# GpSimd's drain moved into the experts' arms, small arms' splits all on VectorE, two weight loads moved behind the first tail's gathers

## The chip, the cores and the metric

The kernel runs on one core of a Trainium2 chip. Its engines are TensorE (PE in the profile, with its weight loads as PEld), VectorE (DVE), ScalarE (ACT), GpSimd (POOL) and SyncE (SP, which only issues DMAs here). Each engine works through its own list of instructions in order and waits for the others by semaphores. The metric is the device time of one execution in microseconds (us); lower is better.

## The reference

Attention over 8 batches and 8 heads (512 local and 32 global positions, a window of 32 on either side) gives 4352 token rows of 512 numbers. A mixture of eight experts then works on them:

```
do_compute = x @ w_skip > 0
xc = x[do_compute];  logits = xc @ w_gate;  e_idx = argmax(logits)
gate_w = softmax(logits)[e_idx]
for e in range(8):
    h = maximum(xc[e_idx == e] @ w1[e], 0)          # 512 -> 1024
    y[e_idx == e] = gate_w * (h @ w2[e])            # 1024 -> 512
out = x.copy();  out[do_compute] = xc + y
```

With the inputs drawn, 1980 tokens are computed, and the experts 0 to 7 get 395, 171, 153, 289, 173, 371, 253 and 175 of them.

## The kernel before, in words

**Attention and routing** take the first 230 us or so. Each token's row is written to `out`, and per expert a list of row numbers and gates is written to a table in DRAM (`lst`).

**An expert** takes its tokens in groups of 128 rows. A gather (line 128) is one indirect DMA on GpSimd's queue that fetches 128 rows of 2 KB from `out`; `gather(...)` issues two of them. TensorE turns the rows (`turn_x`, line 221), and multiplies them with w1 (`first` at line 881 for 256 tokens, `first_small` at line 903 for up to 192) into three PSUM banks used in turn, ScalarE and VectorE turning each result into a high and a low part of `hc` (lines 887, 888, 908, 910). Then TensorE multiplies with w2 (`second`, line 920, 24 matmuls for each 128 tokens; `second_small`, line 931). VectorE weighs the result by the gate and adds the row (`weigh`, line 1000), and GpSimd scatters it back to `out` (`scatter`, line 993).

**The weights** come in float32. Each expert's 4 MB are loaded in eight pieces of 512 KB (lines 176 and 179) into a ring of six `raw` tiles. `split` makes a high part on ScalarE (line 192) and a low part by a subtraction (line 195) on VectorE or, for one piece of each small arm, on GpSimd. `roll(e)` splits one piece and issues the next load (`fetch`). Six rolls stand in an expert's first stage (behind its hidden blocks f = 0, 1, 2, 4, 5, 6), two in its second. SyncE does not wait for these places: it issues the loads in order, each as soon as its tile is free.

**The arms.** Each expert from 1 on has two branches. `few` (at most 192 tokens: experts 1, 2, 4 and 7 here) and `wide` (3, 5 and 6; 3 and 5 have over 256 tokens and also run `tail`). Every engine takes the branch by itself, from a count that it has loaded. Where GpSimd skips an arm, it raises the semaphores that the arm's DMAs would have raised (INC_SWDGE_SEM in the profile). Both arms start with `begin` (line 1207): VectorE weighs the last expert's remaining group into the single tile `ylast`, and GpSimd gathers the next expert's rows into the tile which that group has just left. These rows are turned by `turn_next` between the first and the second stage. A wide arm also gathers its own second list into `xgs[2]` for `tail`. Behind the arms come a scatter of `ylast`, `join` and `weigh` for the second group, a scatter of `yo`, the drain of GpSimd (line 1249), and the second stage of the first 128 tokens.

Expert 0 (lines 1139 to 1197) has its own course: the first stage, `second` twice, with the hooks `rest` (line 1029: gathers of its own third group and of expert 1's rows, and up to four weight loads from GpSimd's queue) and `flags` (line 1155: turns the third group, its "first tail"), then its arms.

The order of each engine's instructions is written out by hand (`manual_schedule`), so that each list stands as the code reads.

Of the kernel before, what the change touches and what calls it, by code (L numbers as in the profile page):

```python
# [45 lines left out]
def kernel(  # L46
# [12 lines left out]
    nc = tc.nc  # L59
# [6 lines left out]
    def ps_s(name):  # L66
        return ps.tile([P, 512], F32, tag="s", name=name, bufs=3)
# [4 lines left out]
    def ps_v(name):  # L72
        return ps.tile([P, 512], F32, tag="v", name=name, bufs=2)
# [16 lines left out]
    six = const.tile([P, E, 2, NSUB], U32, name="six")  # L90
# [9 lines left out]
    xs = []  # L100

    def apart(ins, group, *groups):
        i = getattr(ins, "ins", ins)
        for g in groups:
            tc.declare_no_dep(i, group=g, reason="rows are distinct")
        tc.add_to_no_dep_group(group, i)
# [19 lines left out]
    def gather(xg, gidx, nrow=NT):  # L126
        for t in range(NSUB):
            ins = nc.gpsimd.indirect_dma_start(  # L128
                out=xg[:, t, :], out_offset=None, in_=out[0:nrow, :],
                in_offset=bass.IndirectOffsetOnAxis(ap=gidx[:, t:t + 1], axis=0),  # L130
                bounds_check=nrow - 1, oob_is_err=False,
            )
            apart(ins, "gathers", "scatters")
# [70 lines left out]
    weights = [Weights(e) for e in range(E)]  # L204
# [9 lines left out]
    subs = []  # L214
# [532 lines left out]
    with tc.manual_schedule(engines=engines):  # L747
# [18 lines left out]
        prev, old, first = None, None, slice(0, 1)  # L766
# [106 lines left out]
    def first(e, x2, hc, hook=lambda i: None):  # L873
        hl = wq[e]
        xh, xl = x2
        for f in range(NF):
            ph = ps_s("ph")
            i = 0
            for a, bb in (("w1h", xh), ("w1l", xh), ("w1h", xl)):
                for c in range(NC):  # L880
                    nc.tensor.matmul(  # L881
                        ph[:, 0:GRP], hl[a][:, c, f * P:(f + 1) * P], bb[:, c, :],
                        start=i == 0, stop=i == 3 * NC - 1,
                    )
                    i += 1
            hook(("mid", f))
            nc.scalar.activation(hc[:, f, HI:LO], ph[:, 0:GRP], AF.Relu)  # L887
            nc.vector.scalar_tensor_tensor(
                hc[:, f, LO:LO + GRP], ph[:, 0:GRP], 0.0, hc[:, f, HI:LO].bitcast(F32),
                ALU.max, ALU.subtract,  # L890
            )
            hook(f)

    def first_small(e, x2, hc, hook=lambda i: None):
        hl = wq[e]
        xh, xl = x2
        parts = (slice(0, P), slice(LO, LO + P)), (slice(P, SMALL), slice(SMALL, GRP))
        for f in range(NF):
            ph = ps_s("ph")
            i = 0  # L900
            for a, bb in (("w1h", xh), ("w1l", xh), ("w1h", xl)):
                for c in range(NC):
                    nc.tensor.matmul(  # L903
                        ph[:, 0:SMALL], hl[a][:, c, f * P:(f + 1) * P], bb[:, c, 0:SMALL],
                        start=i == 0, stop=i == 3 * NC - 1,
                    )
                    i += 1
            nc.scalar.activation(hc[:, f, 0:SMALL], ph[:, 0:SMALL], AF.Relu)  # L908
            for hi, lo in parts:
                nc.vector.scalar_tensor_tensor(  # L910
                    hc[:, f, lo], ph[:, hi], 0.0, hc[:, f, hi].bitcast(F32),
                    ALU.max, ALU.subtract,
                )
            hook(f)
# [12 lines left out]
    def second_small(e, hc, py):  # L927
        hl = wq[e]
        for f in range(NF):
            for i, bb in enumerate(("w2h", "w2l")):  # L930
                nc.tensor.matmul(
                    py, hc[:, f, P:GRP], hl[bb][:, f, :],
                    start=f == 0 and i == 0, stop=f == NF - 1 and i == 1,
                )
# [57 lines left out]
    def scatter(yo, sidx):  # L992
        ins = nc.gpsimd.indirect_dma_start(  # L993
            out=out, out_offset=bass.IndirectOffsetOnAxis(ap=sidx, axis=0),
            in_=yo, in_offset=None, bounds_check=NT - 1, oob_is_err=False,
        )
        apart(ins, "scatters", "scatters", "gathers")

    def weigh(py, gate, x, yo):
        nc.vector.scalar_tensor_tensor(yo, py, gate, x, ALU.mult, ALU.add)  # L1000
# [7 lines left out]
    with tc.manual_schedule(engines=engines | {mybir.EngineType.SP}):  # L1008
# [12 lines left out]
        xgs = [xfirst]  # L1021
# [29 lines left out]
        def fetch():  # L1051
            for w in weights[1:]:
                if w.loaded < w.n:
                    return w.load()

        def roll(e, eng=nc.vector):
            if e < E:
                weights[e].split(eng)
                fetch()

        def state():
            return [(w.loaded, w.done) for w in weights]
# [17 lines left out]
        def hint(label, value):  # L1080
            tc.mark_branch_hint_location(label, hint=value, engines={PE})

        def skip(label, e):
            tc.mark_branch_hint_location(
                f"{label}{e}", hint="LikelyTaken", engines={PE}
            )

        def more(e):
            return xgs[2], lambda t: lt[:, e, 1, t, 1:2], six[:, e, 1, :]
# [27 lines left out]
        def h_tile():  # L1117
            return fw.tile([P, NF, 2 * GRP], F32R, name="hc", bufs=1)

        def y_tile():  # L1120
            return fw.tile([P, DM], F32, name="ylast", bufs=1)
# [17 lines left out]
        todo = {i: split0 for i in (2, 3, 4, 5)}  # L1139
        todo.update({6: lambda: weights[1].split(nc.vector), 7: places})  # L1140
        todo["mid", 1] = routed
        hc = h_tile()
        first(0, x2, hc, lambda i: todo.get(i, int)())
        todo = {1: lambda: roll(1), 2: lambda: roll(1), 3: rest}
        gate0 = lambda t: lt[:, 0, 0, t, 1:2]
        py = ps_v("py")
        second(0, hc, 0, py, lambda i: todo.get(i, int)())
# [17 lines left out]
        todo = {3: ready, 6: flags}  # L1165
# [6 lines left out]
        with tc.If(mid > 0, label="few0"):  # L1172
            skip("wide", 0)
            weigh(py, gate0(1), xfirst[:, 1, :], yp)
            todo = {i: lambda: roll(1) for i in (4, 5, 6, 7)}
# [18 lines left out]
                tail(0, (hc[:, :, HI:HI + P], hc[:, :, LO:LO + P]))  # L1194
        scatter(yp, six[:, 0, 0, 1:2])
        hint("few1", flag[1])
        before = last, more(0)[1](0), xgs[2][:, 0, :], own

        for e in range(1, E):
            if e + 1 < E:  # L1200
                weights[e + 1].open(wpool if e % 2 else wpool2)
            hc = h_tile()
            yp = y_tile()
            pc = ps_v("pc")
            xg, gate, sidx = xgs[e % 2], lambda t: lt[:, e, 0, t, 1:2], six[:, e, 0, :]

            def begin():
                weigh(*before[:3], yp)
                if e + 1 < E:
                    gather(xgs[(e + 1) % 2], six[:, e + 1, 0, :])  # L1210

            def turn_next():
                if e + 1 < E:
                    turn_x(xgs[(e + 1) % 2], (e + 1) % 2)

            def hooks(*subs):
                todo = {
                    i: lambda eng=eng: roll(e + 1, eng) for i, eng in zip((0, 1, 2, 4, 5, 6), subs)
                }
                return lambda i: todo.get(i, int)()  # L1220

            dve, pool = nc.vector, nc.gpsimd
            at = state()
            with tc.If(num[e] <= SMALL, label=f"few{e}"):
                skip("wide", e)
                begin()
                first_small(e, xs[e % 2], hc, hooks(dve, dve, dve, pool, dve, dve))
                turn_next()
                second_small(e, hc, pc)
            back(at)  # L1230
            with tc.If(num[e] > SMALL, label=f"wide{e}"):  # L1231
                begin()
                gather(xgs[2], six[:, e, 1, :])
                first(e, xs[e % 2], hc, hooks(dve, dve, dve, dve, dve, dve))
                hint(f"many{e}", nc.values_load(
                    many[0:1, e:e + 1], engines=[PE], min_val=0, max_val=1
                ))
                turn_next()
                second(e, hc, 1, pc)
                with tc.If(num[e] > GRP, label=f"many{e}"):  # L1240
                    tail(e, (hc[:, :, P:GRP], hc[:, :, LO + P:LO + GRP]))
            scatter(yp, before[3])
            if e + 1 < E:
                hint(f"few{e + 1}", flag[e + 1])
            yo = yo_tile()
            join(pc, yo, part[0:HQ, e:e + 1])
            weigh(pc, gate(1), xg[:, 1, :], yo)
            scatter(yo, sidx[:, 1:2])
            nc.gpsimd.drain()  # L1249
            todo = {i: lambda: roll(e + 1) for i in (1, 3)}  # L1250
            todo[4] = lambda: count(e + 2)
            py = ps_v("py")
            second(e, hc, 0, py, lambda i: todo.get(i, int)())
            before = py, gate(0), xg[:, 0, :], sidx[:, 0:1]
# [62 lines left out]
```

## Time and profile before

| | |
|---|---|
| median of 3 runs | 486.59 us (482.91 to 487.25) |
| the profiled execution | 490.02 us |
| its span, first to last instruction | 488.3 us |
| mean granted TensorE clock | 0.979 of 2.4 GHz |
| TensorE busy | 446.0 us (91%) |
| VectorE, ScalarE, GpSimd busy | 309.0, 292.4, 217.8 us |

Times in the rows are from the span's start. A row of the timeline gives start, duration, engine, line, operation, tiles (output <- inputs) and count; the bracket is the time that the engine stood idle before it and what ended that. PEclk is the granted clock of TensorE as a share of 2.4 GHz (0.50 is 1.2 GHz). A span of DRAIN on GpSimd's queue is the time for which that queue stood at it. "DMA to landing" is the time from an issue to the data having arrived.

### The profile page before, as it was taken

What the parts mean: (1) busy time and instruction counts of PE and PEld (TensorE: products, weight loads), DVE (VectorE), ACT (ScalarE), POOL (GpSimd) and SP (SyncE); (2) the same over time, 40 slices, a digit from 0 to 9 for tenths busy, and PEclk for the clock granted to TensorE, in tenths of its full rate; (3) what the DMA queues carried; (4) which work ended last, traced back from release to release, by engine and by line L of the source; (5) the groups of instructions that cost most, each with busy time, mean ns of one, the idle gap of its engine ahead of it and who ended that gap; (6) DMA issues with size and microseconds to landing.
All of it is one profiled execution on the core that took longest, in us unless ns stands there. A gap on an engine that the chain in (4) does not pass through costs nothing. (4 is left out here: it accounts for less than half of the span.)

```text
span 488.3 us, 14036 instructions
## 1 busy us (share of the span) xinstructions
PE 446.0 (91%) x4922; PEld 362.5 (74%) x4922; DVE 309.0 (63%) x1286; ACT 292.4 (60%) x891; POOL 217.8 (45%) x221
## 2 busy tenths in 40 slices
PE   7799999999999998989979999889999799989995
PEld 3566767777767676678959797879779588778793
DVE  6887777887788778765834566746336465138421
ACT  5789999999998987765603363726235344244220
POOL 6555666669865867783460131314014140035101
PEclk9999999999999999989998999989999899998998
DMA  8899988879998787203664556647407657043101
GB/s 264 272 321 300 326 283 256 270 254 260 227 312 262 222 255 234 91 21 102 208 168 167 161 188 219 230 139 248 134 9 243 211 172 247 3 152 118 45 4 51
DMA packets 51143, 93.33 MB, mean 191 GB/s; under 512 B 15932, under 2 KB 20284, under 8 KB 51040
## 3 DMA queue, kind: packets, MB, share of 16 engines
q1 hardware_dynamic: 46144, 82.87, 54.3%
q0 software_dynamic: 4896, 9.20, 5.6%
q8 instruction: 51, 0.84, 0.8%
q14 instruction: 52, 0.43, 0.3%
HBM read 80.81 MB, written 14.67 MB: 196 GB/s over the span
## 5 line engine op out<-in xcount | busy, mean ns | idle before, releaser
L406 ACT ACTIVATE prob<-prob,nmx 128x160 f32<-128x160 f32 x256 | 106.2, 417 | 15.8 <-DVE nmx L401 13.9
L436 POOL TENSOR_TENSOR prob<-prob,inv 128x640 f32<-128x640 f32 x64 | 80.2, 1255 | 59.1 <-ACT prob L406 26.8
L920 PE MATMUL py<-w2h,hc 128*128 128x512 f32 x160 | 52.9, 400 | 5.2 <-PEq L1231 1.5
L993 POOL DMA_INDIRECT out_dram<-yo,six x11 | 11.9, 1082 | 95.4 <-DVEq L1099 48.6
L389 PE MATMUL pss<-ks,qs 64*64 64x160 f32 x1024 | 50.2, 303 | 2.3 <-DVE nmx L401 1.9
L389 PEld LDWEIGHTS pss<-ks,qs 64*64 64x64 f32 x1024 | 33.5, 132 | 19.8 <-issue 13.6
L406 ACT ACTIVATION_READ_ACCUMULATOR prob<-prob,nmx 128x1 f32 x256 | 48.1, 188 | 0.0
L520 PEld LDWEIGHTS pv<-ptT,vw 128*64 128x64 f32 x1024 | 38.8, 137 | 10.8 <-ACT ptT L479 3.0
L520 PE MATMUL pv<-ptT,vw 128*64 128x64 f32 (+1 forms) x1024 | 43.2, 237 | 1.8 <-ACT ptT L479 1.4
L195 DVE TENSOR_TENSOR w2l<-raw,w2h 128x1024 fp32r<-128x1024 f32 (+1 forms) x36 | 41.7, 1178 | 2.3 <-ACT w2h L192 2.1
L677 POOL DMA_INDIRECT lst<-dat,slu x34 | 34.0, 1000 | 18.6 <-DVE slu L672 9.9
L920 PEld LDWEIGHTS py<-w2h,hc 128*128 128x128 f32 x160 | 30.2, 189 | 15.1 <-issue 6.9
L908 ACT ACTIVATE hc<-ph 128x192 fp32r<-128x192 f32 x40 | 13.3, 331 | 43.4 <-PE ph L903 26.1
L476 PE MATMUL pst<-ident,prob 128*128 128x128 f32 x256 | 36.7, 283 | 1.8 <-POOL prob L436 1.2
L192 ACT CAST w1h<-raw 128x1024 fp32r<-128x1024 f32 (+1 forms) x36 | 34.0, 949 | 0.3 <-DMA lst<-dat,slu 0.3
L476 PEld LDWEIGHTS pst<-ident,prob 128*128 128x128 f32 x256 | 27.8, 142 | 8.2 <-issue 4.4
L401 DVE CUSTOM_DVE_ANT_0 prob<-pss,m_even 128x160 f32<-128x160 f32 x96 | 28.1, 318 | 8.6 <-PE pss L389 8.5
L192 ACT CAST w2h<-raw 128x1024 fp32r<-128x1024 f32 (+1 forms) x36 | 33.4, 949 | 0.0
L195 DVE TENSOR_TENSOR w1l<-raw,w1h 128x1024 fp32r<-128x1024 f32 x25 | 30.3, 1220 | 4.5 <-ACT w1h L192 4.5
L920 PE MATMUL py<-w2l,hc 128*128 128x512 f32 x80 | 31.8, 397 | 0.0
L128 POOL DMA_INDIRECT xg<-out_dram,six x16 | 18.7, 1168 | 28.9 <-DVE hc L910 13.4
L887 ACT ACTIVATE hc<-ph 128x256 fp32r<-128x256 f32 x32 | 12.2, 384 | 30.3 <-PE ph L881 24.6
(200 smaller groups left out, 1074.4 us busy)
## 6 DMA issues: line engine op xcount, KB each, us to landing
raw<-in_w_dram SPq DMA_DIRECT2D x62, 512.0 KB, 5.0
vw<-in_v_dram SPq DMA_DIRECT2D x32, 512.0 KB, 5.2
ks<-in_kT_dram SPq DMA_DIRECT2D x32, 400.0 KB, 5.2
out_dram<-xr SPq DMA_DIRECT2D x32, 256.0 KB, 3.7
qs<-in_qT_dram SPq DMA_DIRECT2D x31, 256.0 KB, 5.8
vgs<-in_vgl_dram SPq DMA_DIRECT2D x32, 64.0 KB, 6.1
raw<-in_w_dram POOLq DMA_DIRECT2D x2, 512.0 KB
lst<-dat,slu POOLq DMA_INDIRECT x34, 4.7
```

Of the source, the lines that this page charges most:

```text
L128: ins = nc.gpsimd.indirect_dma_start(out=xg[:, t, :], out_offset=None, in_=out[0:nrow, :], in_offset=bass.IndirectOffsetOnAxis(ap=gidx[:, ...
L192: nc.scalar.copy(hi, raw)
L195: eng.tensor_sub(lo, raw, hi.bitcast(F32))
L389: nc.tensor.matmul(banks[odd][head(h ^ odd), j * W:(j + 1) * W], q[head(h), w * QB:(w + 1) * QB], window(k[head(h)], w), start=True, stop= ...
L401: nc.vector.tensor_tensor_reduce(out=pt[:, i, :], in0=banks[odd][:, j * W:(j + 1) * W], in1=m, scale=-0.125, scalar=3.0e38, op0=ALU.add, o ...
L406: nc.scalar.activation(pt[:, i, :], pt[:, i, :], AF.Exp, bias=nmx[:, i:i + 1], scale=-1.0, accum_out=sums[:, i, 0:1],)
L436: nc.gpsimd.tensor_mul(pt[:, sl, :], pt[:, sl, :], inv[:, sl].unsqueeze(2).to_broadcast([P, 4, W]),)
L476: nc.tensor.transpose(pst[:, i * P:(i + 1) * P], pt[:, 4 * hf + i, 0:KW], ident)
L520: nc.tensor.matmul(pv[head(h), j * 96:j * 96 + n], vv[:, w, head(h)], ptT[:, w, h ^ odd, 0:n], start=j == 0, stop=False, skip_group_check= ...
L677: ins = nc.gpsimd.indirect_dma_start(out=lst, out_offset=bass.IndirectOffsetOnAxis(ap=slu[:, t:t + 1], axis=0), in_=dat[:, bs[j], t - 4 * ...
L908: nc.scalar.activation(hc[:, f, 0:SMALL], ph[:, 0:SMALL], AF.Relu)
L920: nc.tensor.matmul(py, hc[:, f, a + t * P:a + (t + 1) * P], hl[bb][:, f, :], start=f == 0 and i == 0, stop=f == NF - 1 and i == 2,)
```

## The change

1. `nc.gpsimd.drain()` no longer stands behind the scatter of `yo` at the end of each expert, but at the end of `begin` in both arms, behind the gathers. In the wide arms the gather of the arm's own second list now comes ahead of that of the next expert's rows.
2. In the small arms the split behind f = 4 is VectorE's like the others; `roll` and `hooks` lose their engine argument.
3. The two rolls in expert 0's second stage only split and no longer load. The loop in `rest` (unchanged) therefore finds four pieces of expert 1 left and issues all four from GpSimd's queue, behind the gathers; before, SyncE issued two of them ahead. Two `fetch()` calls behind expert 0 issue two pieces of expert 2, which before were issued by the first rolls of expert 1's arms; from there on each load is named two rolls earlier.

```diff
-        def roll(e, eng=nc.vector):
+        def roll(e):
             if e < E:
-                weights[e].split(eng)
+                weights[e].split(nc.vector)
                 fetch()
...
-        todo = {1: lambda: roll(1), 2: lambda: roll(1), 3: rest}
+        todo = {i: lambda: weights[1].split(nc.vector) for i in (1, 2)}
+        todo[3] = rest
...
         scatter(yp, six[:, 0, 0, 1:2])
         hint("few1", flag[1])
+        fetch()
+        fetch()
         before = last, more(0)[1](0), xgs[2][:, 0, :], own
...
-            def begin():
+            def begin(wide):
                 weigh(*before[:3], yp)
+                if wide:
+                    gather(xgs[2], six[:, e, 1, :])
                 if e + 1 < E:
                     gather(xgs[(e + 1) % 2], six[:, e + 1, 0, :])
+                nc.gpsimd.drain()
...
-            def hooks(*subs):
-                todo = {
-                    i: lambda eng=eng: roll(e + 1, eng) for i, eng in zip((0, 1, 2, 4, 5, 6), subs)
-                }
-                return lambda i: todo.get(i, int)()
-
-            dve, pool = nc.vector, nc.gpsimd
+            def hook(i):
+                if i in (0, 1, 2, 4, 5, 6):
+                    roll(e + 1)
+
             at = state()
             with tc.If(num[e] <= SMALL, label=f"few{e}"):
                 skip("wide", e)
-                begin()
-                first_small(e, xs[e % 2], hc, hooks(dve, dve, dve, pool, dve, dve))
+                begin(False)
+                first_small(e, xs[e % 2], hc, hook)
                 turn_next()
                 second_small(e, hc, pc)
             back(at)
             with tc.If(num[e] > SMALL, label=f"wide{e}"):
-                begin()
-                gather(xgs[2], six[:, e, 1, :])
-                first(e, xs[e % 2], hc, hooks(dve, dve, dve, dve, dve, dve))
+                begin(True)
+                first(e, xs[e % 2], hc, hook)
...
             scatter(yo, sidx[:, 1:2])
-            nc.gpsimd.drain()
             todo = {i: lambda: roll(e + 1) for i in (1, 3)}
```

GpSimd's list at the start of expert 3, before. The list does not show drains: here one stands behind the scatter of `yo`. `xfirst` is the tile of the next expert's rows, `xg` that of the arm's own second list.

```order
L993 DMA out_dram<-ylast,six 4352x512
L993 DMA out_dram<-yo,six 4352x512
L1075 TENSOR_LOAD cni
L1224 COMPARE_AND_BRANCH
L128 DMA xfirst<-out_dram,six 128x512 x2
L195 TENSOR_TENSOR w1l<-raw_4470,w1h 128x1024
L1224 UNCONDITIONAL_BRANCH
L1224 ISA
L1224 UNCONDITIONAL_BRANCH
L1231 COMPARE_AND_BRANCH
L128 DMA xfirst<-out_dram,six 128x512 x2
L128 DMA xg<-out_dram,six 128x512 x2
```

The same place in the changed kernel; the drain now stands behind the gathers of each arm.

```order
L993 DMA out_dram<-ylast,six 4352x512
L993 DMA out_dram<-yo,six 4352x512
L1075 TENSOR_LOAD cni
L1227 COMPARE_AND_BRANCH
L128 DMA xfirst<-out_dram,six 128x512 x2
L1227 UNCONDITIONAL_BRANCH
L1227 ISA
L1227 UNCONDITIONAL_BRANCH
L1234 COMPARE_AND_BRANCH
L128 DMA xg<-out_dram,six 128x512 x2
L128 DMA xfirst<-out_dram,six 128x512 x2
```

The subtraction left the few arm, and in the wide arm the own list's two gathers stand ahead of the next expert's.

SyncE's list in expert 0's second stage, before, and then in the changed kernel (`lt` are the lists from DRAM, `raw_95` and `raw_96` tiles of the ring).

```order
L122 DMA lt<-lst 128x7x2 x2
L179 DMA raw_95<-in_w_dram 128x2x512
L179 DMA raw_96<-in_w_dram 128x2x512
L1075 TENSOR_LOAD cni
L1075 ISA x2
```

```order
L122 DMA lt<-lst 128x7x2 x2
L1075 TENSOR_LOAD cni
L1075 ISA x2
L1076 TENSOR_LOAD few
L1076 ISA x2
```

The two loads are gone from SyncE there. GpSimd's list in the changed kernel has them behind the gathers:

```order
L1137 MEMSET xg 128x1024 x2
L128 DMA xg<-out_dram,six 128x512 x4
L179 DMA raw_95<-in_w_dram 128x2x512
L179 DMA raw_96<-in_w_dram 128x2x512
L179 DMA raw_97<-in_w_dram 128x2x512
L179 DMA raw_98<-in_w_dram 128x2x512
L993 DMA out_dram<-yo,six 4352x512
```

Before, only the loads of `raw_97` and `raw_98` stood there.

## Rows read from the trace of the kernel before

**Rows 1.** The page, part 1: busy time, share of the span, instructions.

```profile
PE 446.0 (91%) x4922; PEld 362.5 (74%) x4922; DVE 309.0 (63%) x1286; ACT 292.4 (60%) x891; POOL 217.8 (45%) x221
```

**Rows 2.** Timeline of TensorE, experts' stage: rows with an idle time, one of expert 3.

```profile
255.77 0.66 PE L221 MATMUL xt<-ident,xg 128*128 128x128 f32 x4 [2.22 <-DMA xg<-out_dram,six]
...
280.93 0.66 PE L903 MATMUL ph<-xh,w1h 128*128 128x192 f32 x4 [1.28 <-DMA out_dram<-yo,six]
...
318.14 1.09 PE L221 MATMUL xt<-ident,xg 128*128 128x128 f32 x4 [2.13 <-DMA xg<-out_dram,six]
...
342.13 1.03 PE L221 MATMUL xt<-ident,xfirst 128*128 128x128 f32 x8
...
382.65 1.04 PE L221 MATMUL xt<-ident,xg 128*128 128x128 f32 x4 [2.66 <-DMA xg<-out_dram,six]
...
440.67 1.20 PE L881 MATMUL ph<-xh,w1h 128*128 128x256 f32 x4 [2.62 <-DVE hc L888]
```

**Rows 3.** Windows: stretch, length, busy time by engine, granted clock, DMA share, GB/s.

```profile
254.00:262.00 8.00, 6.23 (x38) 5.89 (x39) 3.48 (x12) 1.43 (x4) 2.04 (x3) 0.79 0.98 356
...
438.00:446.00 8.00, 5.38 (x33) 5.33 (x33) 5.68 (x9) 2.37 (x6) 3.95 (x4) 0.79 0.37 123
318.00:321.00 3.00, 2.86 (x9) 2.51 (x10) 0.85 (x2) 0.59 (x1) 0.09 (x1) 0.50 0.12 46
```

**Rows 4.** Line 1249 on GpSimd's queue, experts 1 and 5: duration in ns, start.

```profile
L1249 POOLq DRAIN  x1: 7698/7698/7698, 300.3 to 300.3; - x1
...
L1249 POOLq DRAIN  x1: 8352/8352/8352, 430.1 to 430.1; - x1
```

**Rows 5.** Line 1224 on GpSimd's queue, 438 to 440 us: skipping few6.

```profile
L1224 POOLq INC_SWDGE_SEM  x1: 180/180/180, 439.2 to 439.2; - x1
```

**Rows 6.** Timeline of GpSimd, experts' stage.

```profile
249.78 1.01 POOL L128 DMA_INDIRECT xg<-out_dram,six  x1 [0.30 <-issue]
...
309.40 1.12 POOL L128 DMA_INDIRECT xg<-out_dram,six  x1 [7.64 <-DVE hc L910]
310.83 1.12 POOL L128 DMA_INDIRECT xg<-out_dram,six  x1 [0.31 <-issue]
312.29 2.40 POOL L195 TENSOR_TENSOR w1l<-raw,w1h 128x1024 fp32r<-128x1024 f32 x1 [0.33 <-ACT w1h L192]
...
332.70 1.05 POOL L128 DMA_INDIRECT xfirst<-out_dram,six  x1 [4.38 <-PE ph L881]
...
429.57 1.97 POOL L993 DMA_INDIRECT out_dram<-ylast,six  x1 [0.72 <-DVE yo L1000]
431.84 0.97 POOL L993 DMA_INDIRECT out_dram<-yo,six  x1 [0.30 <-issue]
441.13 1.54 POOL L128 DMA_INDIRECT xg<-out_dram,six  x1 [8.32 <-DVE hc L888]
```

**Rows 7.** Line 993, scatters: 431.5 to 433 us.

```profile
DMA to landing us min/median/max: 6.3/6.3/6.3
```

**Rows 8.** Line 128, gathers: 216 to 220 us.

```profile
DMA to landing us min/median/max: 4.8/4.8/4.8
```

**Rows 9.** Line 128, gathers: 374.5 to 376 us (expert 4's arm).

```profile
DMA to landing us min/median/max: 6.2/6.8/7.4
```

**Rows 10.** Timeline of VectorE, experts' stage.

```profile
304.26 0.75 DVE L1000 SCALAR_TENSOR_TENSOR ylast<-py,lt,xg 128x512 f32<-128x512 f32 x1 [2.22 <-PE py L920]
...
308.39 1.22 DVE L195 TENSOR_TENSOR w1l<-raw,w1h 128x1024 fp32r<-128x1024 f32 x1
...
313.57 2.19 DVE L195 TENSOR_TENSOR w2l<-raw,w2h 128x1024 fp32r<-128x1024 f32 x1 [0.52 <-ACT w2h L192]
...
439.54 0.75 DVE L1000 SCALAR_TENSOR_TENSOR ylast<-py,lt,xg 128x512 f32<-128x512 f32 x1 [7.73 <-DMA xg<-out_dram,six]
```

**Rows 11.** Timeline of SyncE's queue, 249 to 251 us.

```profile
249.32 1.02 SPq L179 DMA_DIRECT2D raw<-in_w_dram  x2
```

**Rows 12.** Timeline of ScalarE, 265.6 to 266 us: the first cast behind these loads.

```profile
265.73 1.04 ACT L192 CAST w2h<-raw 128x1024 fp32r<-128x1024 f32 x1
```

## The prediction

> **What bounds the kernel now.** I read the busy table first. TensorE is busy 91% of the span [rows 1], so time can come only out of its idle spells, out of its clock, or out of its work; the change leaves its work alone. Then I read TensorE's timeline through the experts' stage, for rows with an idle time. Four stand out [rows 2]: 2.22 us in expert 0's second stage, 2.13 us in expert 2, 2.66 us in expert 4, all three before turning gathered rows, and 2.62 us in expert 6, for an `hc` that VectorE delivers late. Then the windows around these spells [rows 3]. The granted clock falls to 0.50, which is 1.2 GHz, just behind each of them: the mean over 8 us is 0.79, so (1 - 0.79) x 8 = 1.68 us of full-speed time go. The windows at experts 2 and 4 read the same 0.79. Behind the idle of 1.28 us [rows 2] the clock did not fall.
>
> Next, why the rows come late. GpSimd stands 7.70 us at the drain behind expert 1 and 8.35 us at the one behind expert 5 [rows 4]. The one of expert 5 begins at 430.1 and ends at 438.5; only then does GpSimd reach expert 6's branches and raise the semaphores of the arm that it skips, at 439.2 [rows 5]. GpSimd's own work there is short: the scatters of `ylast` and `yo` end at 431.54 and 432.81 [rows 6]. The second of them landed 6.3 us after its issue [rows 7], at 438.1, so the drain's end fits the landing and not the end of the issuing. In expert 2 the drain has ended at 308.0 and the gather starts at 309.40 [rows 4, 6].
>
> **Part 1, the drain.** In the few arms a gather needs the tile that `weigh` leaves. The landings to work with are 4.8 us on quiet queues [rows 8] and up to 7.4 us beside weight loads [rows 9]. In expert 2 that `weigh` runs from 304.26 to 305.01 [rows 10]. In expert 6, where VectorE comes last, it ends at 440.29 and the gather starts at 441.13 [rows 6, 10], 0.84 us later. So the gathers could start at 305.9 and 307.3, the step being 1.43 us [rows 6], and land between 310.7 and 314.7. TensorE wants the second at 316.0 (318.14 - 2.13) in today's course, where the first came about half a microsecond late, so from 315 on. The idle of 2.13 us goes at either end. Expert 4 has the same form, so its 2.66 us go as well.
>
> Expert 6: its `weigh` starts at 439.54 after 7.73 us of waiting [rows 10], 0.3 us behind the raised semaphore. The wide arm reads the tile that the skipped few arm would have gathered into, so it waits for GpSimd to pass. Without the drain GpSimd passes about 1.1 us behind its scatter (438.5 to 439.54 today), at 433.9. Next in line is the landing of the scatter of the single `ylast`, issued at 429.57 [rows 6]; with 4.8 to 7.4 us it is down between 434.4 and 437.0. TensorE has three banks and stopped only at 438.05 (440.67 - 2.62), and `weigh`, `hc` take 1.2 us. At 434.4 there is no idle, at 437.0 just about none. I take the idle of 2.62 us as gone. In experts 3 and 5 TensorE did not wait, so their drains were hidden and give nothing. What the drain holds up in its new place is GpSimd's next scatter, which comes only behind the arm's end.
>
> Idle 2.13 + 2.66 + 2.62 = 7.41 us, clock 3 x 1.68 = 5.04 us; together **12.45 us**. Bounds: 0, if the wait stays, and 12.45.
>
> **Part 2, the splits.** GpSimd's subtraction takes 2.40 us [rows 6], VectorE's 1.22 us, but the one beside it took 2.19 us [rows 10]. VectorE so gains 0.97 and pays 1.22 us in each of experts 1, 2 and 4: +0.25 us each, hidden behind TensorE's blocks; without that cover 0.75 us in all. I take 0. The Trainium skill speaks against this part: "Perfetto Trace Analysis", section Optimizing Scalar/DVE Operations, says that offloading from a saturated VectorE, even to GpSimd, may make sense, with the warning that the two share an SBUF port. The trace bears out the warning, and the rule alone would put 3 x 1.22 = 3.7 us on VectorE and make the sum that much smaller if all of it reached TensorE.
>
> **Part 3, the two loads.** SyncE issues 1 MB at 249.32 [rows 11], while the gather that TensorE waits for was issued at 249.78 [rows 6]; TensorE got on at 255.77, which bounds its landing by 6.0 us. With the loads behind the gathers I give it the quiet 4.8 us [rows 8]: 254.6 instead of 255.8, **1.2 us**. Bounds: 0 and the whole 2.22. The idle left is 1.0 us, less than the 1.28 behind which the clock held, so I count **1.68 us** for the clock too; bounds 0 and 1.68. "DMA: Bandwidth & Descriptors", section Anatomy of one DMA — SWDGE (gpsimd) path, of the Trainium skill gives 2.0 us plus bytes over 436 GB/s, an estimate of 2.6 us for these 256 KB; by it the whole 2.22 us would go and the sum be 1.0 us larger. The quiet rows read 4.8 us, so I stay with them.
>
> In their new place GpSimd spends its queue on the loads, 0.5 us each by SyncE's row and up to 1.4 by a gather's step [rows 6, 11]; the scatter of the first group starts 1 to 3 us later, and its tile is used again only in the arm behind. The pieces are split from 265.73 on [rows 12], some 12 us behind their issue, and a gather beside loads took 7.4. The two `fetch()` calls cost nothing: SyncE issues a load when its tile is free, and that is set by the splits, not by the place in the program.
>
> **The sum**: 12.45 + 1.2 + 1.68 = 15.3 us against the profiled execution of 490.02, so 474.7. The median of the three runs lies 3.4 us below that execution, so I forecast 486.59 - 15.3 = **471.3**, rounded to 471.
>
> **The rivals.**
>
> *A, expert 6 keeps its wait* (chance 0.13). The scatter of `ylast` lands at 437 or later, or the own list's two gathers, now 2.9 us ahead of the next rows (2 x 1.43), make these late at `turn_next`. For it: GpSimd is free only at 432.81, 0.8 us ahead of that arm. Against: the 4.8 us. The gain loses 2.62 + 1.68: about 475.5.
>
> *B, the clock falls anyway* (0.12). TensorE is rated by what it did before, and I know falls only behind idles of 2.1 us or more; smaller ones remain. Then only 7.41 + 1.2 = 8.6 us go: 478.
>
> *C, the drain is not the gate* (0.08). The gathers would be held by something that ends as late, such as the landing of the scatter ahead on the same queue. Against: in expert 1 no drain stands ahead of the gathers, and TensorE did not wait for them. Only part 3 is left: about 484, or 486 without its clock.
>
> *D, slower* (0.05). C, and with it the new order in the wide arms: GpSimd comes to the arm as now, at 332.70 in expert 3 [rows 6], and the next rows' second gather is the fourth, at 332.70 + 3 x 1.43 = 337.0. It lands between 341.8 and 344.4; TensorE turns at 342.13 [rows 2], so up to 2.3 us idle and 1.68 us of clock in each of the three wide arms, 12 us: 498. It decides where that gather lands later than 342.13 in expert 3's course.
>
> *E, more than forecast* (0.07). Part 3 takes the whole idle, or expert 1's 1.28 us shrink too: 466 to 468.
>
> **How the numbers follow.** The forecast, 467 to 474, has 0.55. The range runs from 466 to 479: it takes in A and B and most of E, and leaves out C and D and a rest, under 0.2. One per cent is 4.9 us, about what a measurement of this kernel tells from no change. Faster by more than that: forecast, A, B and E, 0.87. Within it: C, 0.08. Slower: D, 0.05.
>
> **What would show it.** Right: TensorE's rows at turning in experts 2 and 4 and behind the third block of expert 6 have no idle time, and the granted clock is 1.00 there; the gathers of the few arms start within 1 us of the `weigh`; the drains are no shorter, but nothing waits behind them; the subtraction behind f = 5 in the small arms takes about 1.2 us. Part 3: an idle of about 1 us before the first tail's second turning. I am wrong if gathers start more than 3 us behind `weigh`, if a wide arm's turning waits for its rows, or if the clock falls at these four places as before.

## The result

The changed kernel took **469.86 us** (median; 468.60 to 470.62), the kernel before 486.53 beside it: a ratio of **0.9669, 95% interval 0.9617 to 0.9722**, or 16.7 us less. The forecast was 471 and the range 466 to 479. The profiled execution of after has a span of 466.9 us.

The page of after, part 1, with the columns of [rows 1]:

```profile
PE 436.1 (93%) x4922; PEld 354.5 (76%) x4922; DVE 309.2 (66%) x1289; ACT 292.4 (63%) x891; POOL 209.6 (45%) x220
```

TensorE has the same instructions and 9.9 us less busy time: its mean granted clock was 0.998, before 0.979. TensorE's timeline of after, at the places of [rows 2] (turning in expert 0's second stage, expert 1's first block, turning in experts 2 and 4, expert 6's fourth block):

```profile
250.32 1.03 PE L221 MATMUL xt<-ident,xg 128*128 128x128 f32 x8
...
274.81 0.66 PE L903 MATMUL ph<-xh,w1h 128*128 128x192 f32 x4 [1.27 <-DMA raw<-in_w_dram]
...
307.75 1.04 PE L221 MATMUL xt<-ident,xg 128*128 128x128 f32 x8
...
367.20 1.04 PE L221 MATMUL xt<-ident,xg 128*128 128x128 f32 x8
...
420.83 0.63 PE L881 MATMUL ph<-xh,w1h 128*128 128x256 f32 x4
```

The four idles are gone; the 1.27 us at expert 1 stayed. The windows of after around these places, columns as in [rows 3]:

```profile
249.00:257.00 8.00, 7.96 (x59) 6.98 (x58) 4.54 (x15) 2.03 (x5) 6.06 (x7) 1.00 0.84 292
300.00:308.00 8.00, 8.00 (x74) 8.00 (x74) 7.50 (x16) 6.63 (x12) 0.64 (x1) 1.00 0.88 274
360.00:368.00 8.00, 8.00 (x75) 8.00 (x74) 7.50 (x18) 6.52 (x12) 0.10 (x1) 1.00 0.91 315
418.00:426.00 8.00, 8.00 (x71) 8.00 (x70) 6.10 (x9) 6.39 (x11) 3.12 (x3) 1.00 0.78 250
```

The clock reads 1.00 in each, where before read 0.79 at the same four places. The drains did not get shorter. Line 1216 on GpSimd's queue in after, all arms together (shortest, median, longest in ns), answers to [rows 4]:

```profile
L1216 POOLq DRAIN  x7: 3188/4882/7897, 274.6 to 437.5; - x7
```

What changed is what stands behind them. VectorE's `weigh` in expert 2 of after, and then GpSimd's gather:

```profile
297.25 0.75 DVE L1000 SCALAR_TENSOR_TENSOR ylast<-py,lt,xg 128x512 f32<-128x512 f32 x1 [1.17 <-PE py L920]
```

```profile
298.27 1.05 POOL L128 DMA_INDIRECT xg<-out_dram,six  x1 [3.72 <-DVE ylast L1000]
```

The gather starts 0.27 us after `weigh` has ended. Before, the gap was 4.4 us [rows 6, 10].

### The profile page after: what moved, and what is told of

Same layout as the page of the kernel before. It is cut to its first block, busy times and chain, and to the rows that moved or that the text cites. A ratio compares the mean times of both kernels' runs of the same rounds, so it can differ in the third digit from the quotient of the medians.

```text
span 466.9 us, 14036 instructions
## 1 busy us (share of the span) xinstructions
PE 436.1 (93%) x4922; PEld 354.5 (76%) x4922; DVE 309.2 (66%) x1289; ACT 292.4 (63%) x891; POOL 209.6 (45%) x220
## 5 line engine op out<-in xcount | busy, mean ns | idle before, releaser
L406 ACT ACTIVATE prob<-prob,nmx 128x160 f32<-128x160 f32 x256 | 106.2, 417 | 15.6 <-DVE nmx L401 13.8
L436 POOL TENSOR_TENSOR prob<-prob,inv 128x640 f32<-128x640 f32 x64 | 80.3, 1256 | 58.7 <-ACT prob L406 26.8
L993 POOL DMA_INDIRECT out_dram<-yo,six x11 | 13.4, 1217 | 96.9 <-DVEq L1099 57.1
L677 POOL DMA_INDIRECT lst<-dat,slu x34 | 34.4, 1011 | 16.7 <-DVE slu L672 8.0
L195 DVE TENSOR_TENSOR w2l<-raw,w2h 128x1024 fp32r<-128x1024 f32 (+1 forms) x36 | 39.0, 1101 | 2.6 <-ACT w2h L192 2.3
L195 DVE TENSOR_TENSOR w1l<-raw,w1h 128x1024 fp32r<-128x1024 f32 x28 | 34.0, 1219 | 6.3 <-ACT w1h L192 5.4
L908 ACT ACTIVATE hc<-ph 128x192 fp32r<-128x192 f32 x40 | 13.2, 331 | 39.7 <-PE ph L903 21.0
L993 POOL DMA_INDIRECT out_dram<-ylast,six x8 | 8.0, 998 | 47.5 <-DVEq L1234 35.4
L401 DVE CUSTOM_DVE_ANT_0 prob<-pss,m_odd 128x160 f32<-128x160 f32 x96 | 28.3, 320 | 0.0
```

The costliest lines, as they stand in the source:

```text
L195: eng.tensor_sub(lo, raw, hi.bitcast(F32))
L401: nc.vector.tensor_tensor_reduce(out=pt[:, i, :], in0=banks[odd][:, j * W:(j + 1) * W], in1=m, scale=-0.125, scalar=3.0e38, op0=ALU.add, o ...
L406: nc.scalar.activation(pt[:, i, :], pt[:, i, :], AF.Exp, bias=nmx[:, i:i + 1], scale=-1.0, accum_out=sums[:, i, 0:1],)
L436: nc.gpsimd.tensor_mul(pt[:, sl, :], pt[:, sl, :], inv[:, sl].unsqueeze(2).to_broadcast([P, 4, W]),)
L677: ins = nc.gpsimd.indirect_dma_start(out=lst, out_offset=bass.IndirectOffsetOnAxis(ap=slu[:, t:t + 1], axis=0), in_=dat[:, bs[j], t - 4 * ...
L993: ins = nc.gpsimd.indirect_dma_start(out=out, out_offset=bass.IndirectOffsetOnAxis(ap=sidx, axis=0), in_=yo, in_offset=None, bounds_check= ...
```

## Where the time went, by expert

The time of an expert is taken on TensorE's timeline, from the start of its first block to that of the next expert. These spans (us) are read so from the profiled execution of each kernel:

| kernel | expert 2 | expert 4 | expert 6 | expert 7 to the end |
|---|---|---|---|---|
| before | 26.7 | 27.1 | 28.7 | 26.0 |
| after | 22.3 | 22.3 | 24.2 | 26.1 |
| drain_only | 22.3 | 22.8 | 24.2 | 26.0 |
| loads_only | 22.4 | 26.8 | 30.7 | 26.1 |
| splits_only | 27.0 | 28.0 | 24.3 | 26.0 |
| warm_wait | 24.7 | 25.2 | 29.0 | 26.0 |
| drain_13 | 22.3 | 25.2 | 24.3 | 26.1 |
| drain_5 | 22.5 | 22.3 | 28.9 | 26.1 |
| no_drain | 22.4 | 24.1 | 26.1 | 30.4 |
| two_drains | 22.3 | 23.9 | 24.3 | 26.2 |
| early_drain | 22.3 | 25.5 | 29.0 | 26.0 |

From before to after, experts 2, 4 and 6 give 4.4, 4.8 and 4.5 us, and the first tail 3.6 (from TensorE's restart in expert 0's second stage, at 249.86 before and 248.12 after, to expert 0's narrow arm: 7.56 us and 3.96). The two profiled executions differ by more, 21.4 us. 1.7 us of the rest is another fall of the clock ahead of the change, in before alone; some 2.5 us lie in the narrow arm of expert 0 (0.8), expert 1 (0.9) and experts 3 and 5 (0.4 each). How far single executions scatter, warm_wait shows, whose edit begins in expert 2: its expert 1 took 22.3 us, where before's took 23.1, and its expert 0 from the restart on 8.7, where before's took 7.6. So a difference of about a microsecond in this table shows nothing by itself. Windows of before and of after for the stretch with the other fall:

```profile
215.00:250.00 35.00, 33.21 (x304) 29.97 (x304) 22.38 (x69) 17.62 (x38) 15.42 (x16) 0.95 0.40 116
```

```profile
215.00:250.00 35.00, 33.22 (x310) 29.61 (x310) 22.44 (x71) 17.62 (x38) 17.48 (x17) 1.00 0.43 124
```

The last idle ahead of that fall was shorter than any of the four of [rows 2], and the same idle stands in after, where the clock held. TensorE's timeline of before and of after:

```profile
214.74 1.54 PE L569 MATMUL pr<-idw,xT 128*128 128x137 f32 x8 [1.16 <-DVE ptT L479]
```

```profile
214.61 1.20 PE L569 MATMUL pr<-idw,xT 128*128 128x137 f32 x8 [1.16 <-DVE ptT L479]
```

## The experiments

The first four ran on one chip, where the kernel before took 488.45 us; the next four (drain_13, drain_5, no_drain, old_order) and the last four on two others (498.99 and 498.63). Each ratio is to the kernel before on the same chip. The changed kernel itself did not run on the second of these chips: the four runs there are set against its ratio on the third (0.9727, after_again) and against old_order, which ran on the same chip (484.48 us).

**drain_only**: the kernel before with the drain moved and the wide arms' gathers reordered, nothing else.

```diff
+                if wide:
+                    gather(xgs[2], six[:, e, 1, :])
...
+                nc.gpsimd.drain()
...
-            nc.gpsimd.drain()
```

> The kernel before with part 1 alone: the drain at the end of both arms' start, the wide arms' own gather first; GpSimd keeps its split, SyncE its two loads. My theory: the idle spells of TensorE in experts 2, 4 and 6 go with the clock behind them, 12.45 us of 486.5, so 474; the idle of 2.22 us in expert 0 stays. Rival, the drain is not the gate: 486.5, with gathers still starting more than 3 us behind the weigh. Rival, the parts need each other: between 478 and 484.

474.68 us, ratio 0.9717 (0.9684 to 0.9750): 13.8 us, against 12.45 forecast. All three experts lose their wait, and the first tail keeps its own (25.7 us for expert 0 up to its narrow arm, 25.5 in before).

**loads_only**: the kernel before with the two loads behind the first tail's gathers.

```diff
-        todo = {1: lambda: roll(1), 2: lambda: roll(1), 3: rest}
+        todo = {i: lambda: weights[1].split(nc.vector) for i in (1, 2)}
+        todo[3] = rest
...
+        fetch()
+        fetch()
```

> The kernel before with part 3 alone: two weight loads go from SyncE's queue ahead of the first tail's gathers to GpSimd's queue behind them, two fetches behind expert 0. My theory as predicted: 1.2 us of idle and 1.68 us of clock, 483.6; by the trace of the changed kernel, where that idle is gone wholly, 2.22 + 0.70 + 1.68 = 4.6 us, 481.9. Experts 2, 4 and 6 keep their idle spells. Rival, the moved loads only lengthen another wait (the splits of expert 1's last four pieces): 486.5 or more.

483.62 us, ratio 0.9880 (0.9837 to 0.9924): 5.9 us by the ratio, 4.8 by the medians. Its profile shows 3.2 us at the first tail and, unforeseen, expert 2's wait gone as well: the drain ahead of it ended 2.9 us into the expert (302.24), in before 4.0. Expert 6 took 2 us more; the clock gives 1.7 of it (its mean is 0.72 over the 12 us from 432, in before 0.86 over those from 438).

**splits_only**: the kernel before with the small arms' subtraction on VectorE.

```diff
-                first_small(e, xs[e % 2], hc, hooks(dve, dve, dve, pool, dve, dve))
+                first_small(e, xs[e % 2], hc, hooks(dve, dve, dve, dve, dve, dve))
```

> The kernel before with part 2 alone: the small arms' fourth split on VectorE. My theory: hidden, 486.5 within 1 us; VectorE's subtraction behind f = 5 takes 1.2 us in place of 2.2. Rival, VectorE becomes the bound in the small arms: 3 x 1.22 us more, 490.2. Rival, GpSimd's subtraction held up the drain or the gathers: a gain of 2 us or more.

485.34 us, ratio 0.9946 (0.9919 to 0.9974): a small gain where none was expected. In its profile experts 2 and 4 keep their waits and expert 6 has lost it. GpSimd's scatters behind expert 5 show how close that is. GpSimd's timeline of splits_only, then VectorE's of splits_only and of before:

```profile
429.10 0.99 POOL L993 DMA_INDIRECT out_dram<-ylast,six  x1 [0.46 <-issue]
430.39 0.98 POOL L993 DMA_INDIRECT out_dram<-yo,six  x1 [0.31 <-issue]
```

```profile
429.25 2.41 DVE L195 TENSOR_TENSOR w2l<-raw,w2h 128x1024 fp32r<-128x1024 f32 x2
```

```profile
429.45 2.35 DVE L195 TENSOR_TENSOR w2l<-raw,w2h 128x1024 fp32r<-128x1024 f32 x2
```

VectorE's last splits began just behind the first of these scatters; in before they began just ahead of it (429.57), and it took 1.97 us [rows 6]. The next scatter left at 431.84 in before and at 430.39 here; SyncE's weight loads were issued from 431.94 on in before and from 431.78 here. It landed 6.3 us behind its issue in before [rows 7] and 3.0 here, and the drain was 8.35 and 3.81 us long. So some 0.5 us of difference ahead of that point went with 4.4 us in expert 6. That the loads were what held the scatter up fits these times, but no run moved the loads alone; and that the splits bring the difference about regularly is not shown (two of the twelve runs took 488.65 and 489.17 us).

**warm_wait**: the kernel before with 11 matmuls of ones, read by nothing, ahead of `turn_next` in the few arms of experts 2 and 4. It fills the wait and does nothing about the rows, so it is to price the clock alone.

```diff
+                if e in (2, 4):
+                    idle = ps_t("idle")
+                    for _ in range(11):
+                        nc.tensor.matmul(
+                            idle, ones, ones.unsqueeze(1).to_broadcast([P, 4, P]),
+                            start=True, stop=True,
+                        )
                 turn_next()
```

> The kernel before, with 11 bf16 matmuls of 128x512 on constants (some 2.4 us, their result unused) ahead of the turning in the few arms of experts 2 and 4, where TensorE waits for the gather. The wait for the rows stays, TensorE is only busy during it. My theory, that the fall of the clock behind an idle spell costs 1.68 us each: the clock stays at 1.00 in both arms and the time falls by 3.4 us, to 483. Rival, the clock falls anyway or the second-stage work does not feel it: 486.5. Rival, the added matmuls delay the turning more than the rows do: 487 to 490.

486.03 us, ratio 0.9950 (0.9926 to 0.9974), 2.4 us less, where 3.4 were expected. Its fillers and its windows around the waits:

```profile
314.96 2.55 PE L1231 MATMUL idle<-ones 128*128 128x512 bf16 x11
...
377.20 2.55 PE L1231 MATMUL idle<-ones 128*128 128x512 bf16 x11
```

```profile
317.00:325.00 8.00, 7.45 (x37) 5.82 (x36) 4.05 (x8) 3.56 (x5) 1.04 (x1) 1.00 0.62 210
380.00:388.00 8.00, 7.16 (x33) 5.49 (x32) 3.69 (x6) 3.65 (x5) 1.03 (x1) 1.00 0.65 208
```

The clock stayed at 1.00 in both, and experts 2 and 4 took 2.0 and 1.9 us less (3.9 us in the profiles, more than the 2.4 of the medians). Not all of that is the clock, for the rows came a little earlier too: the second turning began 13.53 and 13.99 us into the expert, in before 14.08 and 14.32. From there to the expert's end it took 11.14 and 11.20 us, in before 12.60 and 12.74. So of each wait's price of 4.4 to 4.8 us about 1.5 is the clock: the 1.68 of the sum was near. One profile stands behind it; that the fillers were what held the clock is likely, not shown, since behind 2.24 us of idle in early_drain (below) it held without any.

**drain_13** and **drain_5**: the changed kernel with a second drain at the old place, behind experts 1 and 3, or, with `(5,)` in the edit, behind expert 5.

```diff
             scatter(yo, sidx[:, 1:2])
+            if e in (1, 3):
+                nc.gpsimd.drain()
```

> The changed kernel, with a drain back behind the scatter of yo of experts 1 and 3 (ahead of the small arms 2 and 4), beside those in the arms. My theory: the waits for the gathers come back in experts 2 and 4 with their clock, 2.13 + 2.66 + 2 x 1.68 = 8.2 us above 469.9, 478. Rival, the gathers were late for another reason than the drain (GpSimd's subtraction, the order of the loads): 469.9. Between: the wait comes back without the clock, 474.7.

> The changed kernel, with a drain back behind the scatter of yo of expert 5 alone (ahead of the wide arm 6). My theory: GpSimd reaches the skipped arm some 5 us later, VectorE's weigh waits for it, and TensorE stands 2.6 us behind the third block, with its clock 4.3 us in all: 474.2. Rival, the weigh waits for the landing of the ylast scatter or for the gathers and not for GpSimd to pass: 469.9.

Drain_5: 489.81 us, ratio 0.9836 (0.9776 to 0.9896), 5.4 us above the changed kernel (0.9727), 5.3 above old_order. The wait is back at its place, in the same form as [rows 2]:

```profile
439.32 0.74 PE L881 MATMUL ph<-xh,w1h 128*128 128x256 f32 x4 [3.43 <-DVE hc L888]
```

The clock, though, did not fall behind it in this execution. The window, columns as in [rows 3]:

```profile
437.00:445.00 8.00, 5.68 (x47) 5.68 (x48) 6.79 (x10) 2.02 (x5) 4.18 (x4) 1.00 0.39 101
```

Expert 6 lost 4.7 us here by waiting alone.

Drain_13: 489.59 us, ratio 0.9827 (0.9765 to 0.9888): 5.0 us above the changed kernel, where 8.2 were expected. In its profile only expert 4 pays (2.9 us, with 1.08 and 1.46 of idle at turning); **expert 2 pays nothing**, though a drain stands ahead of its gathers again. That execution was the fastest of four (487.15 to 493.04 us); what the slower ones paid is not on record. Its two drains at the old place, line 1252:

```profile
L1252 POOLq DRAIN  x2: 3750/5452/7154, 307.9 to 368.7; - x2
```

The one of expert 1 lasted 3.75 us, not 7.70 [rows 4], and was over as expert 2 began. So the drain's place alone does not explain expert 2's wait in the kernel before: its length counts as well.

**no_drain**: the changed kernel without any drain.

```diff
-                nc.gpsimd.drain()
```

> The changed kernel without any drain in the experts. My theory: the drains in the arms hold up nothing that is waited for, 469.9 within 1 us. Rival, they still hold up GpSimd (scatters, skipped arms): a gain of 1 us or more. Rival, they keep GpSimd from running ahead to a worse place: slower.

494.48 us, ratio 0.9922 (0.9891 to 0.9953): 9.7 us **slower** than the changed kernel by the ratios, 10.0 slower than old_order. The theory that nothing needs the drain fell. Three views show why. First, the step that raises semaphores for the tail arm that is passed over, line 1099 in no_drain and then in after:

```profile
L1099 POOLq INC_SWDGE_SEM  x2: 1375/1483/1591, 367.3 to 429.1; - x2
```

```profile
L1099 POOLq INC_SWDGE_SEM  x2: 197/197/197, 351.8 to 411.2; - x2
```

Without drains this step grows through the program, from 1.14 us at 286.6 to 1.74 at 460.5. Second, GpSimd's timeline of no_drain behind expert 3's end, and VectorE's:

```profile
369.76 2.03 POOL L993 DMA_INDIRECT out_dram<-ylast,six  x1 [1.80 <-issue]
```

```profile
376.17 0.75 DVE L1000 SCALAR_TENSOR_TENSOR ylast<-py,lt,xg 128x512 f32<-128x512 f32 x1 [5.24 <-issue]
```

The scatter of the single `ylast` comes 1.2 us later than in after, falls beside VectorE's splits, takes 2.03 us (1.00 in after), and `weigh`, which reuses `ylast`, starts 4.1 us into expert 4 (0.2 in after). Experts 4 and 6 lose 1.8 us each. Third, the drains with which the program ends, no_drain and after:

```profile
L1313 POOLq DRAIN  x3: 46/109/7985, 482.3 to 490.9; - x3
```

```profile
L1314 POOLq DRAIN  x3: 46/109/3112, 462.4 to 466.6; - x3
```

4.9 us more, with nothing to hide it. In no_drain that drain ended at 490.31, and all DMA queues from 484.9 to 490.3 read:

```profile
DMA  0000000000000000000000000000000000000000
GB/s 0 0 0 0 0 0 0 0 0 0 0 0 0 0 0 0 0 0 0 0 0 0 0 0 0 0 0 0 0 0 0 0 0 0 0 0 0 0 0 0
DMA packets 2, 0.00 MB, mean 0 GB/s; under 512 B 2, under 2 KB 2, under 8 KB 2
```

Everything had landed 5.4 us earlier. So a drain goes on behind the last landing, and for how long fits the number of transfers that GpSimd had issued since the drain before (the last packet is that of GpSimd's own queue):

| drain | transfers since the last drain | end behind the last packet, us |
|---|---|---|
| after, at the program's end | 3 | 0.5 |
| after, expert 2 | 5 | 0.55 |
| two_drains, expert 6 | 29 | 1.65 |
| before, expert 1 | 48 | 2.56 |
| no_drain, at the program's end | 81 | 5.4 |

Between the rows that is 44 to 62 ns for each further transfer. What the engine does in that time no row says, and whether the count of transfers sets it, or something that grows with it, is not separated.

**old_order**: the changed kernel with the wide arms' gathers in the old order, next rows first.

```diff
-                if wide:
-                    gather(xgs[2], six[:, e, 1, :])
                 if e + 1 < E:
                     gather(xgs[(e + 1) % 2], six[:, e + 1, 0, :])
+                if wide:
+                    gather(xgs[2], six[:, e, 1, :])
```

> The changed kernel, with the wide arms' gathers in the order of before (the next expert's rows first, then the arm's own list). My theory: no wait of TensorE hangs on either, 469.9 within 1 us. Rival, the own list first is what makes the wide arms 0.4 us shorter in the changed kernel's trace (experts 3 and 5): 470.7. Rival, the next rows first save a wait: faster.

484.48 us, ratio 0.9713 (0.9660 to 0.9766): not told apart from the changed kernel's 0.9727, so nothing shows that the order mattered.

**after_again**: the changed kernel, unedited, as the base of the last group.

> The changed kernel once more, unedited, beside the next ones on one chip. Every theory: 0.967 of the kernel before (0.962 to 0.972). It is the base of the next runs.

485.47 us, ratio 0.9727 (0.9704 to 0.9749): 13.2 us less than before, against 16.7 in the result, and just outside the 0.962 to 0.972 that was expected. On this chip the first tail stops elsewhere, and the loads' place does not help there: expert 0 up to its narrow arm took 25.8 and 26.0 us. After_again, then early_drain, which has the loads at the old place:

```profile
262.28 0.61 PE L920 MATMUL py<-w2h,hc 128*128 128x512 f32 x1 [2.95 <-DVE yo L1000]
```

```profile
261.89 0.50 PE L920 MATMUL py<-w2h,hc 128*128 128x512 f32 x1 [2.83 <-DVE yo L1000]
```

**two_drains**: the changed kernel with its drain in the arms of experts 1 and 6 alone.

```diff
-                nc.gpsimd.drain()
+                if e in (1, 6):
+                    nc.gpsimd.drain()
```

> The changed kernel with its drain kept in the arms of experts 1 and 6 alone. Theory (a drain settles the account of all earlier GpSimd transfers, 62 ns each, and without it INC_SWDGE_SEM costs 1.1 to 1.7 us and the drain that ends the program 8.0 us in place of 3.1): two are enough. INC_SWDGE_SEM stays under 0.8 us behind expert 1, the last drain is under 4 us, the time is that of the changed kernel within 1.5 us, some 8 us under the kernel without drains. Rival (each arm's drain holds GpSimd back from running ahead to a worse place, expert by expert): experts 4 and 6 lose 1.8 us each as without drains, and the time lies 4 us or more above the changed kernel.

486.35 us, ratio 0.9740 (0.9716 to 0.9764): 0.9 us above the changed kernel, within the intervals, and 9 below no_drain by the ratios. The last drain is 3.20 us, and line 1099 reads between the two kernels:

```profile
L1099 POOLq INC_SWDGE_SEM  x2: 395/503/611, 368.0 to 429.2; - x2
```

So nearly all of no_drain's loss goes with the transfers that no drain has yet settled; some of it (1.6 us in expert 4 of this profile) comes back as their number grows again.

**early_drain**: the kernel *before* with one more drain, in expert 0's narrow arm, where GpSimd is idle.

```diff
+            nc.gpsimd.drain()
             turn_x(xgs[1], 1)
             xg, gate, sidx = more(0)
```

> The kernel before with one more drain, on GpSimd inside expert 0's narrow arm, where GpSimd stands idle for over 20 us. Theory (of the 7.70 us of expert 2's drain, 2.56 us come behind its last packet and settle 48 earlier transfers): expert 2's drain ends within 0.8 us of its last packet, its turning waits up to 2.6 us less, and the time falls by 2 to 4 us (ratio 0.992 to 0.996). Rival (a drain is as long as its last landing): its length and the time stay as they are, 1.000.

494.03 us, ratio 0.9921 (0.9898 to 0.9945): 3.9 us less for one line. Expert 2's wait is gone with its drain still in place; the profile of before that is compared below comes from another chip. Its drain behind expert 1 and its turning in expert 2:

```profile
L1250 POOLq DRAIN  x1: 6667/6667/6667, 308.9 to 308.9; - x1
```

```profile
323.38 1.04 PE L221 MATMUL xt<-ident,xg 128*128 128x128 f32 x8
```

The drain ends 2.9 us into expert 2, not 4.0, and 0.8 us behind its last packet, not 2.56. The gather starts 1.1 us earlier in the expert. Before, its packets began 0.6 us behind the issue of SyncE's next weight load and the two gathers took 5.8 and 7.2 us; here they began 0.3 us ahead of that issue, and nothing waits. Expert 4's wait is still here, but the clock held behind it. TensorE's timeline and its window, columns as in [rows 3]:

```profile
386.91 0.63 PE L221 MATMUL xt<-ident,xg 128*128 128x128 f32 x4 [2.24 <-DMA xg<-out_dram,six]
```

```profile
385.00:393.00 8.00, 5.56 (x25) 4.37 (x26) 3.27 (x7) 2.44 (x5) 1.03 (x1) 1.00 0.59 176
```

**after_early**: the changed kernel with the same line added, the candidate for a better one.

> The changed kernel with the same additional drain in expert 0's narrow arm, the candidate for a better one. INC_SWDGE_SEM ahead of expert 1 falls from 1.14 to under 0.5 us and expert 1's drain from 6.75 to about 4.5 us; nothing on TensorE waits for either in the changed kernel, so by the theory the time is the same within 1 us. By the rival that GpSimd's run into expert 1 is late by that clean-up, 1 to 2 us faster.

485.03 us, ratio 0.9730 (0.9711 to 0.9749): the same time as the changed kernel. The semaphore step ahead of expert 1 fell to 0.23 us and expert 1's drain to 4.92, and nothing had waited for either. No run beat the changed kernel beyond its interval.

## Why the prediction was right, step by step

**Part 1, the drain** (12.45 us): right in place and nearly in size, 13.8 by drain_only. The sum left out the short idles ahead of the first turnings, 0.46 us in expert 2 and 0.17 in expert 4. The rows named as proof came out: no idle at turning, gathers behind `weigh` within 0.3 us, drains no shorter. For expert 6 the gather of the own list even starts at 416.06, ahead of `weigh` at 416.31. Drain_5 puts expert 6's wait back. Two parts of the reasoning were too simple. The drain was read as as long as the last landing; that holds for expert 5 (438.1 and 438.5), but ahead of expert 2 the last packet was over at 305.46 and the drain went on for 2.56 us, with 48 transfers since the drain before. With fewer, the drain's old place cost expert 2 nothing in the profiles of drain_13 and early_drain. And a transfer was taken to be late by as much as its gate; in experts 2 and 6 about 1 to 1.5 us of lateness went with waits that cost over 4, the transfers running beside weight loads. That the loads made the rest is argued from the times, not shown.

**The clock** (3 x 1.68, and 1.68 at the first tail): right in size; warm_wait's profile gives 1.46 and 1.54 us in experts 2 and 4. The reading behind it, and behind rival B, that the clock falls behind idles of 2.1 us or more, does not hold: it fell behind 1.16 us at 214.74 of before, and not behind the same 1.16 in after, 2.24 in early_drain or 3.43 in drain_5. That it fell at all four places in the one profile from which the sum was made is in part luck.

**Part 2, the splits** (0): in the whole change nothing of it is seen. Alone it measured a ratio of 0.9946, where the term said 1; what its profile shows is expert 6's scatter slipping ahead of the loads, a wait that the moved drain removes anyway. The changed kernel with the split back on GpSimd was not measured. The subtraction behind f = 5 took 1.21 us, as forecast (306.70, expert 2), and the 0.25 us on VectorE are hidden as said. The Trainium skill ("Perfetto Trace Analysis", Optimizing Scalar/DVE Operations) speaks of offloading from a saturated VectorE; this one was busy 63% [rows 1], and no run here shows the 3.7 us on TensorE.

**Part 3, the loads** (1.2 + 1.68): the term of 1.2 was too small. All 2.22 us went, and with it an idle of 0.70 us ahead of the first turning that the sum left out; no idle is left at 250.32, and the first tail gave 3.2 to 3.6 us. The step that failed is the landing of 4.8 us that was taken for quiet queues [rows 8]: in after, the gather that the first tail waits for last landed in 2.8 us, and expert 2's two in 3.3 and 4.0. The Trainium skill's estimate ("DMA: Bandwidth & Descriptors", Anatomy of one DMA, SWDGE path) of 2.6 us is nearer to the shortest of them, 2.8; before, expert 2's gathers took 5.8 and 7.2 us beside loads, far from it.

**The sum.** 15.3 was forecast and 16.7 came; that the two lie so near is in part luck, since on the third chip the same change gave 13.2 and part 3 nothing that its profile shows. The parts alone measured ratios of 0.9717, 0.9880 and 0.9946, whose product is 0.955; the whole is 0.967. They do not add, and the profiles show why: the parts remove the same waits. Expert 2's goes with the drain or with the loads, expert 6's with the drain or in splits_only. Of the rivals, A, B, C and D did not come; D's mechanism, the order of the wide arms' gathers, makes no difference (old_order). E's first half did. C's second price comes to 485.4 by its own terms (486.59 - 1.2), not 486.

What stays open: why the first tail stops for `yo` on the two other chips; why expert 1 is 0.9 us shorter in some executions, that of warm_wait among them, whose edit comes only behind it; what decides whether the clock falls behind an idle; and whether the splits move expert 6's scatter in every execution.

## What to carry to other kernels

Put a drain where its engine would be idle and nothing else is queued behind it, and do not drop it because nothing seems to need it: here seven hidden drains saved 9.7 us over none. When a wait is longer than the lateness of what releases it, look at what the late transfer now runs beside; here 0.5 us (expert 6) and 1.1 us (expert 2) ahead of a burst of loads went with over 4 us each. Do not count on a fall of the clock behind every idle, nor on its holding behind a short one: take it from the window. Parts that remove the same wait do not add, so measure them alone and together.

## What the hardware showed that was not expected

- A GpSimd drain ended later behind the last packet the more transfers that engine had issued since the last drain: 0.5 us with 3, 2.56 with 48, 5.4 with 81, some 45 to 60 ns for each.
- `INC_SWDGE_SEM` grows with the same count: 0.16 us just behind a drain, 1.14 with 46 transfers since, 1.74 with 79 at the end of no_drain, about 20 ns for each.
- A scatter issued 0.12 us after a VectorE split had begun took 1.97 us on GpSimd, one issued 0.15 us before such a split 0.99.
- Where TensorE's wait was filled with matmuls that nothing reads, the clock stayed at its upper level, and the stage behind the wait was 1.46 and 1.54 us shorter.
- The length of one idle did not tell whether the clock would fall: it fell behind 1.16 us (before, 214.74) and held behind the same 1.16 (after, 214.61), behind 2.24 (early_drain, 386.91) and behind 3.43 (drain_5, 439.32).
